# Attention and gated FFN on one core: slots by inner tile with four accumulators open, two batches in turns at the start, one order by hand

## The chip, the cores and the metric

The kernel runs on one core of a Trainium2 chip. The metric is the device time of one execution in microseconds (us). Engines are called as in the profile: PE does matmuls (PEld loads their weights), DVE is the vector engine, ACT the scalar engine, POOL the general one, SP issues most DMAs.

## What is computed

Eight batches of eight heads, 576 tokens of 64 elements, 32 memories per head, then a feed-forward part on all 4608 tokens with model width 512 and inner width 2048:

```python
a = exp(phi - max(phi)); a = a / (sum(a) + 1e-09)
k_m = einsum('bhsm,bhsd->bhmd', a, k)
v_m = einsum('bhsm,bhsd->bhmd', a, v)
scores = (q @ k_m^T) / 8
attn = softmax(scores)                 # with + 1e-09 in the sum
x = (attn @ v_m) as (4608, 512)
h = x @ w_in
out = (h * clip(h + 3, 0, 6) / 6) @ w_out
```

The two weight matrices reach the core as 64-bit floats.

## The kernel before

**Tiles.** A batch is handled in two halves (hf) of 256 and 320 tokens. The inner width is cut into 16 tiles f of 128; four of them are a chunk c of w_in (w1), and w_out (w2) has one piece per tile. Per batch the attention makes the memories (`pk`), turns them (`pq`), makes scores (`psc`) and probabilities (`phi`, `plo`: high and low part). `fold` (L308) multiplies the value memories with a chunk of w1 into `pv`, and `unload` (L325, L326) splits this into high and low parts, `both`, two tiles f at a time.

**A slot** is one half and one tile f: `gemm1` (L357) makes `ph` with six matmuls; `gate` makes `gf` (ACT L370, then DVE L371, with a 64-column piece for tokens beyond 256, L374, kept in `rest`), then its high part `ghi` (ACT L377) and low part `glo` (DVE L384); `gemm2` (L398) adds six products with w2 to two accumulators `acc`. gemm2 runs two slots behind gemm1 (LAG = 2). On the second half of every second batch, the kept 64-token pieces of two batches make a third tile, `rboth`, with three more matmuls a slot and a third accumulator. There are two PSUM buffers for `ph`, four for `acc` and one pair for the attention.

**Weights.** Each piece of 128 x 512 double words becomes 32-bit floats: ACT makes the size and shifts the low word (L95, L96), DVE clamps, shifts and masks (L102 to L104), POOL adds the integers (L105). A w2 piece is then split into high (ACT L110) and low (POOL L111). Converted chunks of w1 are written to DRAM (`w1_kept`) and fetched back for later batches.

**Order.** The last seven batches stand in an order written by hand: all 16 tiles of the first half, then of the second, and the next batch's attention steps at fixed slots, run as `aside` between ghi and glo. The first batch is different. Only SP's loads are in a fixed order there (`FETCH`). `SCRIPT` (attention and first weights) and `PLAN` (slots, weight pieces by `tick`, steps of batch 1) say in which order the work is recorded, and a scheduler with an estimate of times decides how it stands on each engine. It runs the first batch as four rows of eight slots: each half over tiles 0 to 7, kept as partial sums in DRAM, then each over 8 to 15. Batch 1's slots follow when batch 0 is finished.

Of the kernel before, what the change touches and what calls it, by code (L numbers as in the profile page):

```python
# [33 lines left out]
PLAN = ('0.0 13 C1 w2 - - / 0.1 - w3 E1 / 0.2 / 0.3 w4 / 0.4 F1 D1 / 0.5 w5 w6 / 0.6 B1 R1 - w7 21 / 0.7 - / 1.0 23 / 1.1 - 20 - 22 - / 1.2 / 1.3 / 1.4 / 1.5 w8 w9 - / 1.6 31 - - / 1.7 30 F2 - w11 32 - 33 S - / 2.8 / 2.9 S w10 w12 F3 / 2.10 S S / 2.11 - / 2.12 S S - w13 - S - S S S / 2.13 S - w14 w15 G0 / 2.14 S - - / 2.15 S / 3.8 / 3.9 S / 3.10 - G1 G2 S S S / 3.11 - / 3.12 / 3.13 G3 S - S S / 3.14 / 3.15'
)
SCRIPT = ('maxima / tick 00 01 / exponents / memories (0,1) / memories (2,3,4) / normalise / turn / scores 0 / centre 0 / tick 02 03 - / exponent 0 / divide 0 / tick w0 w1 / tick 10 @scores0 / back 0 / tick 12 @divide0 / tick 11 @centre0 / rest 0 / scores 1 @back0 / fold 0'
)
FETCH = ('pt 00 k2 k0 pn k1 k3 01 03 k4 02 w0 q0 w1 10 11 13 q1 w2 20 12 w3 w4 w6 w11 w5 w9 23 w10 w7 21 22 w8 31 30 w15 32 w12 w14 33 w13'
)
HOT = lambda hf: hf == 0  # L40
GLO = lambda ch, f: False
# [9 lines left out]


@with_exitstack
def attention_ffn_kernel(ctx: ExitStack, tc: tile.TileContext, pn, pt, kv, qt, w1, w2, out):
# [30 lines left out]

    def halves(raw):
        words = raw.bitcast(U32).rearrange("p (n t) -> p n t", t=2)
        return words[:, :, 0], words[:, :, 1]  # L90

    def begin(raw):
        low, high = halves(raw)
        tmp = sb.tile([P, DM], U32, name="tmp", **TMP)
        nc.scalar.activation(tmp.bitcast(F32), high.bitcast(F32), AF.Abs)  # L95
        nc.scalar.activation(low, low, AF.Copy, scale=2.0**-29)  # L96
# [2 lines left out]
    def join(raw, tmp, dst):
        low, high = halves(raw)  # L100
        size = tmp.bitcast(F32)
        nc.vector.tensor_scalar(size, size, LOW, TOP, ALU.max, ALU.min)  # L102
        nc.vector.tensor_scalar(tmp, tmp, 3, 0x3FFFFFF8, ALU.logical_shift_left, ALU.bitwise_and)  # L103
        nc.vector.scalar_tensor_tensor(high, high, 0xC0000000, tmp, ALU.bitwise_and, ALU.bitwise_or)  # L104
        nc.gpsimd.tensor_tensor(tmp if dst is None else dst, high, low, ALU.add)  # L105

    def split(f, full):
        w2_sb[f] = wpool.tile([P, 2, DM], F32R, name=f"w2_{f}", tag=f"w2_{f}")
        hi, lo = w2_sb[f][:, 0], w2_sb[f][:, 1]
        nc.scalar.copy(hi, full)  # L110
        nc.gpsimd.tensor_tensor(lo, full, hi.bitcast(F32), ALU.subtract)  # L111
# [549 lines left out]
```

## Time and profile before

| | |
|---|---|
| time, median of 3 runs | 765.0 us (763.57 to 766.19) |
| the profiled execution | 766.2 us |
| its span | 764.3 us |
| busy: PE / DVE / ACT / POOL | 701.9 / 440.6 / 369.3 / 119.5 us |
| bytes read / written in HBM | 86.52 / 14.69 MB |

A page of the profile comes from one execution. Times in a row are the start from the beginning of the span and the duration; in a group's row the total busy time and the mean of one in ns, then how long the engine stood idle before these instructions, and what ended that. An fp32 matmul shows as two instructions. `L` numbers are lines of the kernel; the changed kernel's lines are other ones.

### The profile page before, as it was taken

How to read it: one execution, taken by the hardware profiler on the slowest of the kernel's cores; microseconds unless marked ns; L12 is line 12 of the kernel's file. 1: busy time of each engine (PE TensorE's matmuls, PEld its weight loads, DVE VectorE, ACT ScalarE, POOL GpSimd, SP SyncE). 2: the span in 40 equal slices, each digit the busy share in tenths (PEclk: the TensorE clock that was granted, in tenths of full speed). 3: DMA queues.
4: the chain of work that ended last, by engine and by line, in shares of the span. 5: the costliest groups of instructions: out<-in, count | busy, mean ns of one | idle time of the engine just before them, and what ended most of it. 6: DMA issues, size and time to landing. Idle time of an engine off the chain costs nothing.

```text
span 764.3 us, 12420 instructions
## 1 busy us (share of the span) xinstructions
PE 701.9 (92%) x4690; PEld 563.4 (74%) x4690; DVE 440.6 (58%) x1033; ACT 369.3 (48%) x823; POOL 119.5 (16%) x99
## 2 busy tenths in 40 slices
...
PEclk9559999999999999999999999999999999999999
...
GB/s 324 409 406 48 283 169 277 140 257 12 248 109 86 97 111 194 117 106 45 240 93 85 97 139 195 108 95 69 227 77 82 152 3 82 56 28 1 29 1 41
DMA packets 28442, 102.00 MB, mean 133 GB/s; under 512 B 4960, under 2 KB 5856, under 8 KB 24288
## 3 DMA queue, kind: packets, MB, share of 16 engines
...
q8 instruction: 37, 0.61, 0.3%
...
HBM read 86.52 MB, written 14.69 MB: 132 GB/s over the span
## 4 chain that ended last, share of the span: by engine, by line
PE 79%; DMA 8%; DVE 8%; issue 2%; ACT 2%; POOL 1%; SPq 0%; POOLq 0%; DVEq 0%; ACTq 0%
PE acc L398 48%; PE ph L357 24%; PE pv L308 3%; DMA raw<-in_w 3%; PE pk L225 2%; DVE raw L104 2%; DVE tmp L102 1%; DMA kvt<-in_kv 1%; DMA nmx<-nmx 1%; PE psc L254 1%; DVE tmp L103 1%; DMA w<-w_kept 1%; DVE glo L384 1%; DMA ptile<-in_pt 1%; POOL w L105 1%
## 5 line engine op out<-in xcount | busy, mean ns | idle before, releaser
L398 PE MATMUL acc<-w,ghi 128*128 128x512 f32 x1024 | 288.7, 401 | 0.8 <-POOL w L111 0.6
L370 ACT ACTIVATE gf<-ph,three 128x320 f32<-128x320 f32 (+1 forms) x256 | 128.0, 500 | 200.1 <-PE ph L357 195.6
L371 DVE SCALAR_TENSOR_TENSOR gf<-gf,ph 128x256 f32<-128x256 f32 x256 | 107.0, 418 | 199.0 <-ACT gf L370 198.4
L398 PEld LDWEIGHTS acc<-w,ghi 128*128 128x128 f32 x1024 | 178.7, 189 | 54.4 <-ACT gf L370 23.2
L357 PEld LDWEIGHTS ph<-phi,both 128*128 128x128 f32 x1024 | 165.4, 191 | 54.6 <-DVE gf L371 15.8
L357 PE MATMUL ph<-phi,both 128*128 128x320 f32 (+1 forms) x1024 | 182.6, 300 | 23.0 <-DVE gf L371 11.2
L377 ACT CAST ghi<-gf 128x256 fp32r<-128x256 f32 x256 | 104.0, 406 | 144.5 <-DVE gf L371 144.3
L398 PE MATMUL acc<-w,glo 128*128 128x512 f32 x512 | 165.4, 399 | 1.9 <-DVE glo L384 1.9
L384 DVE TENSOR_TENSOR glo<-gf,ghi 128x256 fp32r<-128x256 f32 x256 | 114.1, 447 | 48.3 <-ACT ghi L377 47.1
L398 PEld LDWEIGHTS acc<-w,glo 128*128 128x128 f32 x512 | 95.6, 189 | 28.7 <-DVE glo L384 3.7
L357 PE MATMUL ph<-plo,both 128*128 128x320 f32 (+1 forms) x512 | 110.4, 297 | 0.0
L357 PEld LDWEIGHTS ph<-plo,both 128*128 128x128 f32 x512 | 83.3, 191 | 0.0
L273 POOL TENSOR_TENSOR st<-st,mx 128x640 f32<-128x640 f32 (+1 forms) x15 | 18.5, 1235 | 387.0 <-DVE mx L272 387.0
L326 DVE TENSOR_TENSOR both<-pv,both 128x512 fp32r<-128x512 f32 x64 | 44.1, 689 | 45.8 <-ACT both L325 45.7
L398 PE MATMUL acc<-w,rboth 128*128 128x512 f32 x192 | 54.9, 394 | 0.0
L308 PE MATMUL pv<-w,kvT 64*32 64x512 f32 x512 | 39.7, 629 | 8.7 <-DVE st L263 5.8
L398 PEld LDWEIGHTS acc<-w,rboth 128*128 128x128 f32 x192 | 36.1, 188 | 9.0
L325 ACT CAST both<-pv 128x512 fp32r<-128x512 f32 x64 | 37.1, 580 | 5.5 <-DVE both L326 4.9
L225 PE MATMUL pk<-kvt,pnat 128*32 128x129 f32 (+1 forms) x640 | 22.1, 289 | 9.4 <-DVE pnat L215 4.4
L104 DVE SCALAR_TENSOR_TENSOR raw<-raw,tmp 128x512 uint32<-128x512 uint32 x32 | 30.5, 957 | 0.3
L225 PEld LDWEIGHTS pk<-kvt,pnat 128*32 128x32 f32 (+1 forms) x640 | 18.2, 115 | 12.8 <-ACT pnat L216 5.1
L95 ACT ACTIVATE tmp<-raw 128x512 f32<-128x512 f32 x32 | 21.1, 674 | 13.1 <-DMA raw<-in_w 7.7
...
## 6 DMA issues: line engine op xcount, KB each, us to landing
...
```

The lines of the kernel that those rows point to most:

```text
L95: nc.scalar.activation(tmp.bitcast(F32), high.bitcast(F32), AF.Abs)
L104: nc.vector.scalar_tensor_tensor(high, high, 0xC0000000, tmp, ALU.bitwise_and, ALU.bitwise_or)
L225: nc.tensor.matmul(self.pk[j * M : (j + 1) * M, g, :KV], self.pnat[:rows, t, g * P + j * M : g * P + (j + 1) * M], kvt[:rows, g * NJ + j, ...
L308: nc.tensor.matmul(pv[j * M : (j + 1) * M, g, :], self.kvT[rows, g, j * M : (j + 1) * M], w1_sb[c][rows, j, :].bitcast(F32), start=True, s ...
L325: nc.scalar.copy(vhi, pv[:, :, x : x + VC])
L326: nc.vector.tensor_tensor(vlo, pv[:, :, x : x + VC], vhi.bitcast(F32), ALU.subtract)
L357: nc.tensor.matmul(ph, w[:, g, fs], x[:, g * n : (g + 1) * n], start=(i == 0), stop=(i == len(seq) - 1),)
L370: nc.scalar.activation(gf, ph, AF.Relu, bias=three)
L371: nc.vector.scalar_tensor_tensor(gf[:, :n], gf[:, :n], 6.0, ph[:, :n], ALU.min, ALU.mult)
L377: nc.scalar.copy(ghi, gf[:, :n])
L384: nc.vector.tensor_tensor(glo, gf[:, :n], ghi.bitcast(F32), ALU.subtract)
L398: nc.tensor.matmul(accs[a], lo if i == 2 else hi, w2lo if i == 1 else w2hi, start=(first and i == 0), stop=(last and i == 2),)
```

## The change

1. **Slots by inner tile.** From batch 2 on, a batch runs tile by tile, both halves of a tile after each other (`pairs`), so that two halves of two accumulators are open at once. LAG is 3. The third accumulator is gone: after every second batch a `rest_segment` of its own makes eight double tiles of the kept pieces, with one accumulator.
2. **First two batches in turns.** Batch 0 runs tiles 0 to 3 half by half (FIRST, 8 slots), batch 1 tiles 0 to 3 half by half and 4 to 7 in pairs (SECOND, 16 slots), batch 0 tiles 4 to 15 (THIRD, 24 slots), batch 1 tiles 8 to 15 (FOURTH, 16 slots). The partial sums of both batches go to DRAM and come back (`keep`, `recall`).
3. **One order by hand.** The whole kernel stands under `manual_schedule`: each engine gets its instructions in the order in which the code records them. A table names the work of each slot's aside; `begin`, `size`, `join` and `split` are the steps of a weight unit, `unfold` is one half of unload.
4. **Weight units of 1024 columns** in place of pieces of 512. The integer add is recorded on DVE (`nc.vector`), no longer on POOL. Two buffers `tmp` of 1024 columns take the place of four of 512.
5. **Small things.** Five matmuls without use (`warm`) in the prologue; the second half's scores of batch 0 go to two accumulator buffers (`scoreb`); the transposed scores are read when centre runs; phi, plo and kvT have other buffer counts; output goes out in larger DMAs.

```diff
-LAG = 2
-PLAN = ('0.0 13 C1 w2 - - / 0.1 - w3 E1 / 0.2 / 0.3 w4 / 0.4 F1 D1 / 0.5 w5 w6 / ...
-SCRIPT = ('maxima / tick 00 01 / exponents / memories (0,1) / ...
+LAG = 3
+PROLOGUE = """
+pt.0 raw.0.0 pn.0 kv.0 raw.0.1 q.0.0 raw2.0 max.0 q.0.1 raw2.1
+begin.0.0.0 size.0.0.0 join.0.0.0 exps.0 mem.0 norm.0 turn.0 begin.0.0.1 size.0.0.1
+score.0.0 pt.1 pn.1 kv.1 centre.0.0 exp.0.0 join.0.0.1 scoreb.0.1 q.1.0 warm.4 begin.1.0 div.0.0 back.0.0
+fold.0.0 unfold.0 rest.0.0 warm.1
+"""
+FIRST = """
+0 unfold.0 size.1.0 / 1 join.1.0 split.0 max.1 spread.1 q.1.1 raw2.2 raw2.3 / 2 centre.0.1 exp.0.1
+/ 3 div.0.1 back.0.1 rest.0.1 begin.1.1 / 4 size.1.1 exps.1 / 5 join.1.1 split.1 mem.1
+/ 6 norm.1 turn.1 raw.1.0 raw.1.1 score.1.0 centre.1.0 exp.1.0 fold.1.0
+/ 7 unfold.1 div.1.0 back.1.0 unfold.1 rest.1.0
+"""
+SECOND = """
...
+/ 8 unfold.1 size.1.2 / 9 join.1.2 split.2 begin.1.3 / 10 size.1.3 / 11 join.1.3 split.3 begin.0.2.0
...
+THIRD = """
+0 begin.1.4 / 1 size.1.4 / 2 join.1.4 / 3 split.4 fold.0.2 unfold.0 / 4 unfold.0 begin.0.3.0 / 5 size.0.3.0 / 6 join.0.3.0
...
+    def begin(*u):
+        sizes[u] = sb.tile([P, UNIT], U32, name="tmp", **TMP)
+        for cols, high, part in raw[u]:
+            nc.scalar.activation(sizes[u][:, cols].bitcast(F32), high.bitcast(F32), AF.Abs)
+            nc.scalar.activation(part, part, AF.Copy, scale=2.0**-29)
...
-        nc.vector.scalar_tensor_tensor(high, high, 0xC0000000, tmp, ALU.bitwise_and, ALU.bitwise_or)
-        nc.gpsimd.tensor_tensor(tmp if dst is None else dst, high, low, ALU.add)
...
+            nc.vector.scalar_tensor_tensor(size_, high, 0xC0000000, size_, ALU.bitwise_and, ALU.bitwise_or)
+            nc.vector.tensor_tensor(dst[:, cols], size_, part, ALU.add)
...
+    def split(u):
...
+        nc.scalar.copy(w2_sb[u][:, 0], whole)
+        nc.gpsimd.tensor_tensor(w2_sb[u][:, 1], whole, w2_sb[u][:, 0].bitcast(F32), ALU.subtract)
...
+    def high_low(aside, *sources):
...
+        nc.scalar.copy(ghi, src)
+        aside()
+        nc.vector.tensor_tensor(glo, src, ghi.bitcast(F32), ALU.subtract)
...
+        segment(0, halves(range(4)), table(FIRST, atts), keep)
+        segment(1, halves(range(4)) + pairs(range(4, 8)), table(SECOND, atts), keep)
+        segment(0, pairs(range(4, NFT)), table(THIRD, atts), store)
+        segment(1, pairs(range(8, NFT)), table(FOURTH, atts), store)
+        for b in range(2, B + 1):
+            if b % 2 == 0:
+                rest_segment(b - 1, {})
```

Three places show how the instructions stand on the engines. The first is ACT among the weights of w2: before, in the first batch's slots.

```order
L110 CAST w_5_570<-tmp 128x512
L377 CAST ghi<-gf 128x256
L96 ACTIVATE raw<-raw 128x512
L370 ACTIVATE gf<-ph,three 128x256
L95 ACTIVATE tmp<-raw 128x512
L377 CAST ghi<-gf 128x256
L110 CAST w_6_577<-tmp 128x512
L370 ACTIVATE gf<-ph,three 128x256
```

And now, in slots 9 and 10 of SECOND (relu is L384, ghi L376, split L154, begin L127 and L128):

```order
L384 ACTIVATE gf<-ph,three 128x320
L376 CAST ghi<-gf 128x256
L154 CAST w_2_892<-tmp 128x1024
L127 ACTIVATE tmp<-raw_3_333 128x1024
L128 ACTIVATE raw_3_333<-raw_3_333 128x1024
L384 ACTIVATE gf<-ph,three 128x256
L376 CAST ghi<-gf 128x256
```

Single pieces of 512 columns stood between relu and ghi of several slots; now all of a unit's ACT work stands between one slot's ghi and the next slot's relu. The second place is the beginning of DVE's program, before:

```order
L194 TENSOR_REDUCE nmx<-ptile 128x2
L202 TENSOR_SCALAR diag<-ident,nmx 128x128 x2
L102 TENSOR_SCALAR tmp<-tmp 128x512
L103 TENSOR_SCALAR tmp<-tmp 128x512
L104 SCALAR_TENSOR_TENSOR raw<-raw,tmp 128x512
L215 TENSOR_TENSOR pnat<-pnat,pa 128x512 x2
L215 TENSOR_TENSOR pnat<-pnat,pa 128x256
```

Now (size is L132 and L133, join L145 and L146, the exponents' addition L230):

```order
L209 TENSOR_REDUCE nmx<-ptile 128x2
L217 TENSOR_SCALAR diag<-ident,nmx 128x128 x2
L132 TENSOR_SCALAR tmp<-tmp 128x1024
L133 TENSOR_SCALAR tmp<-tmp 128x1024
L145 SCALAR_TENSOR_TENSOR tmp<-raw,tmp 128x512
L146 ISA w_136<-raw,tmp 128x1024
L145 SCALAR_TENSOR_TENSOR tmp<-raw,tmp 128x512
L146 ISA w_136<-raw,tmp 128x1024
L230 TENSOR_TENSOR pnat<-pnat,pa 128x512 x2
L230 TENSOR_TENSOR pnat<-pnat,pa 128x256
```

Two pieces with their adds stand ahead of the exponents in place of one without; the add of 512 words is listed as an ISA instruction of 1024 elements. The third place is PE at batch 1's memories, before (they stood among batch 0's last tiles):

```order
L357 MATMUL ph<-phi,both 128x256 x2
L357 MATMUL ph<-plo,both 128x256 x2
L225 MATMUL pk<-kvt,pnat 32x129 x40
L357 MATMUL ph<-phi,both 128x256 x4
L357 MATMUL ph<-plo,both 128x256 x2
L398 MATMUL acc<-w_12_1051,ghi 128x512 x4
```

Now, in slots 5 and 6 of FIRST (gemm1 is L361, gemm2 L443, the memories L239):

```order
L361 MATMUL ph<-phi,both 128x320 x4
L361 MATMUL ph<-plo,both 128x320 x2
L239 MATMUL pk<-kvt,pnat 32x129 x40
L443 MATMUL acc<-w_1_437,ghi 128x512 x4
L443 MATMUL acc<-w_1_437,glo 128x512 x2
L361 MATMUL ph<-phi,both 128x320 x4
L361 MATMUL ph<-plo,both 128x320 x2
L259 MATMUL pq<-ident,kvn 128x128 x2
```

The memories moved from the end of batch 0 to its sixth slot, and the acc of tile 2, which reads the second w2 unit, stands ahead of the next ph.

More of the change, by code (lines that the diff above doesn't have):

```diff
@@ L30 @@
 FC = DF // NCHUNK
+FPC = FC // P
+UNIT = 2 * FC
 KV = 2 * D + 1
 EPS = 1e-9
-LAG = 2
[L34 to L41, printed above, removed]
+LAG = 3
 VC = 256
-VW_RING = {"tag": "vw", "bufs": 9}
-TMP = {"tag": "tmp", "bufs": 4}
+VW_RING = {"tag": "vw", "bufs": 6}
+TMP = {"tag": "tmp", "bufs": 2}
+O_RING = {"tag": "o", "bufs": 2}
 WIDE = {"tag": "wide", "bufs": 2}
@@ L99, in join @@
[L99 to L111, printed above, removed]
@@ new lines, in store_rest, with finish @@
+    def store_rest(b, hf, accs):
+        o = sb.tile([P, 2, DM], F32, name="o", **O_RING)
+        half = DM // 2
+        nc.scalar.mul(o[:, 0, :half], accs[0][:, :half], 1.0 / 6.0)
+        nc.vector.tensor_scalar(o[:, 0, half:], accs[0][:, half:], 1.0 / 6.0, None, ALU.mult)
+        for k in range(2):
+            row = (b + k) * S - REST
+            nc.sync.dma_start(out=out[row : row + REST], in_=o[k * REST : (k + 1) * REST, 0])
+    pending = []
+    open_accs = {}
+    def finish(key, tiles, first, last, end):
+        if first:
+            open_accs[key] = [bank() for _ in range(1 + max(t[0] for t in tiles))]
+        accs = open_accs[key]
+        one = len(accs) == 1
+        order = [(k, i) for i in range(3) for k in range(len(tiles))]
+        if not one and last:
+            order.sort()
+        for n, (k, i) in enumerate(order):
+            a, hi, lo, f = tiles[k]
+            w2hi, w2lo = w2_parts(f)
+            opens = n == 0 if one else i == 0
+            closes = n == len(order) - 1 if one else i == 2
@@ L603, in attention_ffn_kernel @@
-    then = ahead(2)
-    with tc.manual_schedule():
-        for b in range(1, B):
-            att, nxt = nxt, then
-            rows, then = timetable(nxt, b + 2)
-            for hf in range(2):
-                def aside(f):
-                    for what in rows[hf * NFT + f]:
-                        what()
-                run(b, hf, range(NFT), store, None, None, None, aside)
+                start=first and opens,
+                stop=last and closes,
+            )
+        if last:
+            end(*key, open_accs.pop(key))
```

504 lines of the change are left out of this document (207 added, 297 removed).

## The prediction

> **What bounds the kernel now.** I read the page first, then the busy time of each engine by stages, then single rows of the stages that matter.
>
> ```profile
> span 764.3 us, 12420 instructions
> PEclk9559999999999999999999999999999999999999
> 0.00:54.00 54.00, 15.80 (x160) 8.11 (x160) 40.58 (x68) 29.57 (x51) 20.70 (x23) 0.67 0.99 381
> 54.00:126.00 72.00, 57.22 (x336) 41.61 (x336) 66.94 (x115) 46.10 (x95) 41.51 (x31) 0.96 0.57 189
> 126.00:185.00 59.00, 54.02 (x429) 40.90 (x423) 37.27 (x82) 26.18 (x60) 11.36 (x9) 0.97 0.60 171
> 270.00:441.00 171.00, 171.00 (x1188) 139.91 (x1192) 90.61 (x232) 81.11 (x186) 15.32 (x12) 1.00 0.43 122
> ```
>
> The columns of a stage are its length, then busy time of PE, PEld, DVE, ACT and POOL, the granted clock, the DMA share and GB/s. From 270 to 441 us PE is never idle at clock 1.00. Before 54 us it works 15.8 us of 54 and at a mean clock of 0.67; from 54 to 126 us DVE is busy 66.9 us of 72 and PE 57.2. So there is a start of some 185 us, short of data first and then of DVE, and after it PE alone sets the pace.
>
> ```profile
> 269.90 2.54 PE L225 MATMUL pk<-kvt,pnat 128*32 128x129 f32 x80
> 440.56 2.54 PE L225 MATMUL pk<-kvt,pnat 128*32 128x129 f32 x80
> 137.12 0.74 PE L357 MATMUL ph<-phi,both 128*128 128x320 f32 x4
> 139.40 0.75 PE L357 MATMUL ph<-phi,both 128*128 128x320 f32 x4
> 158.82 0.64 PE L357 MATMUL ph<-phi,both 128*128 128x256 f32 x4
> 160.93 0.64 PE L357 MATMUL ph<-phi,both 128*128 128x256 f32 x4
> 758.96 0.87 PE L398 MATMUL acc<-w,rboth 128*128 128x512 f32 x3
> ```
>
> Two batches take 440.56 - 269.90 = 170.7 us, so eight at PE's pace take 682.6. The last matmul ends at 759.8, which leaves a tail of 4.5. The start therefore loses 764.3 - 682.6 - 4.5 = **77 us**, and only that can change: the matmuls of the eight batches are the same in number and shape. A slot (one inner tile of one half: six matmuls into ph, six into acc) costs PE 139.40 - 137.12 = 2.28 us with 320 columns and 160.93 - 158.82 = 2.11 with 256, so 2.2 on average; of it the six acc matmuls are about 1.4.
>
> **The change, part by part.** The steady part keeps its folds, attention steps and matmuls; PE hides ACT (81 us of 171) and DVE (91 of 171) there. I cost its new order, the separate rest tiles and the longer delay of three slots at nothing; were that cover gone, each slot could cost up to the 1.35 us that follows below.
>
> What matters is one order written by hand for the start. In it every engine works through its instructions in program order, and one slot's chain is:
>
> ```profile
> 243.88 0.53 ACT L370 ACTIVATE gf<-ph,three 128x320 f32<-128x320 f32 x1 [1.36 <-PE ph L357]
> 244.43 0.42 DVE L371 SCALAR_TENSOR_TENSOR gf<-gf,ph 128x256 f32<-128x256 f32 x1 [1.46 <-ACT gf L370]
> 244.89 0.41 ACT L377 CAST ghi<-gf 128x256 fp32r<-128x256 f32 x1 [0.48 <-DVE gf L371]
> 245.33 0.42 DVE L384 TENSOR_TENSOR glo<-gf,ghi 128x256 fp32r<-128x256 f32 x1 [0.34 <-ACT ghi L377]
> ```
>
> From relu to gf 0.55 us, from there to ghi 0.46; with 0.35 until ACT is free, the next relu can start 1.35 us after the last. A slot's extra work now stands between ghi and the next relu on ACT, and between gf and glo on DVE. So a slot with extra ACT work a takes 1.35 + a, one with extra DVE work d about 0.9 + d (gf, the 64-column piece, glo), and where ACT's extra work waits for DVE's, both add up. A waiting cast holds up the next relu and through it everything on DVE, hence the next ph bank and PE. In the old order weight pieces of 512 columns overlapped freely on ACT, DVE and POOL.
>
> The weight pieces, alone and by group:
>
> ```profile
> 43.18 0.67 ACT L95 ACTIVATE tmp<-raw 128x512 f32<-128x512 f32 x1 [1.17 <-DVE raw L104]
> 43.76 0.66 ACT L96 ACTIVATE raw<-raw 128x512 uint32<-128x512 uint32 x1
> 48.05 0.41 DVE L103 TENSOR_SCALAR tmp<-tmp 128x512 uint32<-128x512 uint32 x1
> 48.39 0.41 DVE L102 TENSOR_SCALAR tmp<-tmp 128x512 f32<-128x512 f32 x1
> 7.70 0.69 DVE L104 SCALAR_TENSOR_TENSOR raw<-raw,tmp 128x512 uint32<-128x512 uint32 x1
> L104 DVE SCALAR_TENSOR_TENSOR raw<-raw,tmp 128x512 uint32<-128x512 uint32 x32 | 30.5, 957 | 0.3
> L105 POOL TENSOR_TENSOR w<-raw 128x512 uint32<-128x512 uint32 x16 | 19.9, 1246 | 36.0 <-DVE raw L104 30.7 <-PE ph L357 4.1 <-ACT st L276 1.1
> L111 POOL TENSOR_TENSOR w<-tmp,w 128x512 fp32r<-128x512 f32 x16 | 23.6, 1479 | 8.3 <-ACT w L110 8.3
> ```
>
> The change converts units of 1024 columns. Back to back, ACT starts a 512-column op every 0.58 us and DVE a tensor_scalar every 0.34. No row shows 1024 columns; one op must lie between one and two halves, and I take nearly two: begin 2.0 us on ACT (2.3 for w1, still in halves), size 1.2 on DVE. The mask-and-or is 0.61 per half back to back. The integer add moves from POOL to DVE as another kind of instruction. No row shows it there: below it is bounded by a 0.41 pass over 512 columns, above by POOL's own 1.25; I take 0.75, near the 0.69 of L104 on the same operands. So join is 2.7 us for w1 and, in one piece, 2.6 for w2. split is 0.95 on ACT and then 2.6 on POOL, under two of L111's 1.48 since one start is saved. Moving the add takes 37 us off POOL and lets DVE's passes run nearer 0.69 than the group's 0.957; I have counted that gain by pricing DVE without POOL beside it.
>
> The beginning, before any slot:
>
> ```profile
> 6.07 0.67 ACT L95 ACTIVATE tmp<-raw 128x512 f32<-128x512 f32 x1 [4.06 <-DMA raw<-in_w]
> 10.45 1.62 DVE L215 TENSOR_TENSOR pnat<-pnat,pa 128x512 f32<-128x512 f32 x3 [2.06 <-DMA pnat<-in_pn]
> 12.28 3.19 PE L225 MATMUL pk<-kvt,pnat 128*32 128x129 f32 x64 [4.42 <-DVE pnat L215]
> 18.33 1.08 PE L225 MATMUL pk<-kvt,pnat 64*32 64x129 f32 x16 [2.87 <-DMA kvt<-in_kv]
> 19.47 0.16 DVE L236 TENSOR_SCALAR rs<-pk 128x2 f32<-128x2 f32 x1 [2.91 <-PE pk L225]
> 22.97 1.11 PE L254 MATMUL psc<-qh,kvT 64*32 64x256 f32 x16 [0.67 <-ACT kvT L247]
> 53.95 0.41 DVE L371 SCALAR_TENSOR_TENSOR gf<-gf,ph 128x256 f32<-128x256 f32 x1
> ```
>
> Now DVE converts half of the first w1 chunk ahead of the exponents. ACT starts its first piece at 6.07 as before, the second lands 1.3 us later (512 KB at 381 GB/s), so size and join run from 7.9 to 12.0, so the exponents start at 12.0 instead of 10.45. But the last key tile no longer waits behind weights, and pk (4.3 us) ends near 17.5 instead of 19.4. From rs to psc 3.5 us less ACT work that went between: psc at 20.1. Then on DVE size to 23.1, transpose, maximum and subtraction to 25, join to 27.7, division to 29.8, transpose to 30.5; phi on ACT, fold, one half of both and plo to 33.7, and the first gf at **34.5** against 53.95 (the old one came after many pieces that could have waited). The warm matmuls run on PE beside that DVE chain. By pk (40 products of 129 columns, four side by side, in 2.54 us: 2.0 ns a column) one is 1.0 us, twice that at half clock; without this cover the four would cost 4 to 8 us.
>
> On SP the start's loads (ptile, half a w1 chunk, pnat, kv, the other half, q, w2 unit 0, q, w2 unit 1: 9 MB, 24 us at 381 GB/s) stand in the order of use and land before it. Behind batch 1's row of maxima and its way through DRAM wait a q and two w2 units, needed over ten slots later; all other pieces are issued at least six slots ahead. I cost SP and DMA at nothing; a piece that came late would hold ACT's begin and so the gate by as much.
>
> Then the slots, priced with these parts. The two halves' attention adds round trips through POOL inside one slot:
>
> ```profile
> L282 DVE TENSOR_REDUCE sm<-st 128x20 f32<-128x640 f32 x8 | 6.5, 811 | 0.5 <-ACT st L276 0.5
> L285 POOL TENSOR_TENSOR st<-st,sm 128x640 f32<-128x640 f32 x8 | 10.3, 1290 | 21.9 <-DVE sm L284 20.5 <-ACT gf L370 1.4
> L289 DVE STREAM_TRANSPOSE pT<-st 128x640 f32<-128x640 f32 x8 | 6.7, 837 | 0.2
> L298 POOL TENSOR_TENSOR plo<-pT,phi 128x640 fp32r<-128x640 f32 x8 | 12.7, 1590 | 16.0 <-ACT phi L292 16.0
> ```
>
> Division and turning back in one slot: 0.34 + 0.81 + 0.45 (the two small ops) + 1.29 on POOL + 0.84 + phi 0.7 + plo 1.59, then the end of ph 0.45 and 0.55 to the next gf: **7.0 us**, since the next half's first ph needs plo. There are three such slots (7.05, 7.8 with two unfolds, 7.0). A slot with norm, turn, score and centre chained through PE takes 7.3.
>
> - FIRST, 8 slots: 3.55 + 4.6 + 4.7 + 7.05 + 4.3 + 9.0 + 7.3 + 7.8 = 48.3. The 9.0 is a join and split (4.7) after which PE's acc of slot 2 waits 4.3 more for POOL's low half of the second w2 unit, ahead of the next ph.
> - SECOND, 16 slots: 3.65, 2.2, 2.75, 7.0, 3.9, 2.05, 3.55, 3.9, 3.55, 6.7, 1.9, 7.0, 1.9, 4.4, 3.55, 3.5 = 61.5. The 6.7 is slot 9: 0.5 + join 2.6 + 0.1 + split 0.95 + begin 2.0 + 0.55.
> - THIRD, slots 0 to 18: six units of w2 and w1 in turns of begin (3.35 to 4.65), size (2.05), join (3.4) or join with split (4.7): 61.0. After slot 18 no weights are left and PE sets the pace.
>
> First gf 34.5 + 48.3 + 61.5 + 61.0 = 205.3 us. PE, which runs ahead of gf by one ph and is behind in acc by one tile, has then done 42 slots (92.2), three more ph (2.4), six folds at 1.33 (8.0, what is left of 170.7 us after slots, rest tiles and attention) and two batches' memories and scores (8.3): 110.9 of the 682.6. The rest follows at PE's pace: 205.3 + 571.7 + 4.5 = **781.5 us** of span, 17 more than before. The profiled execution took 766.2, 1.9 more than its span, and the median shown, 765.0, is 1.2 under that: 781.5 + 1.9 - 1.2 = 782.
>
> **A rule against the change.** The clock row above shows two slices of 19 us at half clock although PE worked in them; later there is one short fall:
>
> ```profile
> 160.00:180.00 20.00, 15.51 (x131) 11.23 (x133) 11.09 (x23) 8.85 (x21) 0.00 (x0) 0.91 0.40 148
> ```
>
> The Trainium skill, "TensorE: Matmul & The Clock Gate", Part 1, says that the clock falls to half after an idle window of about 3.4 us and rises after a busy one. The trace agrees in part: 0.91 over 20 us is 3.6 us at half. By that rule the warm matmuls help once and each wait of 7 us lets the clock fall again, which is the third rival below.
>
> **The rivals.**
> - *DVE and ACT overlap* (faster): if the chain did not add up and each stage took only its DVE work, FIRST would take 31 us (eight gates 7.8, two w2 units 8.8, attention, unfolds and the store 14), SECOND 51, THIRD 57: 173.5 at the end of 48 slots with 119.6 done, so 741 of span, 742 as a median. It is decided where the mean slot up to there falls below 3.6 us (mine is 4.0); for it speaks DVE's 67 of 72 us in the old stage, against it the program order of both engines. Half of that effect would be about no change.
> - *The add is dear*: at 1.25 per half, 28 halves on the path add 14 us: 796. At 0.41 they take 9.5 away: 773. The order lists it with twice its columns, which speaks for dear.
> - *The clock falls at each long wait*: six waits, each followed by about 1.5 slots at double time, cost up to 6 x 2 = 12 us: 794. For it speaks the fall between 160 and 180 us, against it that this one cost only 3.6 us at half clock.
> - *The early start is all*: stalls no larger than before after the first gf, 19 us earlier: 746. Against it: the chain above.
>
> **How the numbers follow.** Forecast near 782 (770 to 790): 0.47. The add or the clock dearer (790 to 806): 0.20. Faster, by overlap or by the early start (738 to 762): 0.27. No change: 0.06. The range from 744 to 800 leaves out half of the dear end and some of the fast one. Within 0.3% (2.3 us) is what a measurement of this kernel tells from no change: faster 0.27, same 0.06, slower 0.67.
>
> **What would show it.** The first gf near 34 us; gf of the 44th slot near 205; PE busy well under half its time from 35 to 80 us; ACT relus released by casts that wait for DVE's add; from about 210 us on the old pace of 170.7 us for two batches. The forecast is wrong if the add is under 0.5 us per half, if the 1024-column ops cost little more than 512, or if slots of the SECOND stage average under 3.2 us.

## The result and the profile after

| | changed | before, on the same chip |
|---|---|---|
| time, median | 817.6 us (816.2 to 818.7) | 764.6 us (763.6 to 766.2) |
| ratio | 1.069, 95% interval 1.066 to 1.072 | |
| span of the profiled execution | 814.3 us | 764.3 us |
| busy: PE / DVE / ACT / POOL | 721.2 / 434.5 / 362.4 / 77.9 us | 701.9 / 440.6 / 369.3 / 119.5 us |

The direction was forecast, the size was not: 782 us, and at most 800. From the page of the changed kernel, its span and the granted clock in 40 slices:

```profile
span 814.3 us, 12199 instructions
PEclk9756888999989999999999999999999999999999
```

The clock is now below nine tenths of full speed not in two slices but in six of the first ten, and in one later. The busy times by stage, changed kernel (length, PE, PEld, DVE, ACT, POOL, granted clock, DMA share, GB/s):

```profile
35.00:80.00 45.00, 25.80 (x170) 16.91 (x169) 21.75 (x41) 15.36 (x29) 10.33 (x6) 0.62 0.43 148
80.00:140.00 60.00, 45.46 (x225) 34.19 (x224) 35.59 (x69) 28.68 (x53) 10.83 (x7) 0.83 0.37 140
140.00:210.00 70.00, 53.33 (x290) 40.59 (x290) 50.67 (x97) 39.31 (x75) 7.63 (x4) 1.00 0.41 142
210.00:255.00 45.00, 33.10 (x251) 26.46 (x252) 22.20 (x51) 15.71 (x36) 2.38 (x1) 0.89 0.47 105
330.00:500.00 170.00, 167.01 (x1150) 137.10 (x1156) 89.14 (x222) 77.95 (x174) 14.21 (x11) 1.00 0.33 112
```

Three things stand in these rows. Up to 140 us no engine is the bound: PE, DVE and ACT all work well under their time, so instructions wait for one another. From 210 to 255, where PE was expected to set the pace, it works 33 of 45 us. And in the steady part it is idle 3 us in 170, where it was never idle before. The gate of the first slot of each table, and of the 44th slot, in the timeline of the changed kernel:

```profile
35.15 0.42 DVE L385 SCALAR_TENSOR_TENSOR gf<-gf,ph 128x256 f32<-128x256 f32 x1 [1.10 <-ACT gf L384]
...
90.39 0.42 DVE L385 SCALAR_TENSOR_TENSOR gf<-gf,ph 128x256 f32<-128x256 f32 x1 [1.11 <-ACT gf L384]
...
153.82 0.41 DVE L385 SCALAR_TENSOR_TENSOR gf<-gf,ph 128x256 f32<-128x256 f32 x1
...
216.16 0.42 DVE L385 SCALAR_TENSOR_TENSOR gf<-gf,ph 128x256 f32<-128x256 f32 x1 [1.21 <-ACT gf L384]
```

So FIRST took 55.2 us (forecast 48.3), SECOND 63.4 (61.5), slots 0 to 18 of THIRD 62.3 (61.0), and the first gate came 0.7 late. The 44th slot came at 216.2 instead of 205.3: 10.9 us of the error. From there to the end it took 598.2 us, where 571.7 + 4.5 were forecast: the other 22.0.

### The profile page after: what moved, and what is told of

Same layout as the page of the kernel before. It is cut to its first block, busy times and chain, and to the rows that moved or that the text cites. A ratio compares the mean times of both kernels' runs of the same rounds, so it can differ in the third digit from the quotient of the medians.

```text
span 814.3 us, 12199 instructions
## 1 busy us (share of the span) xinstructions
PE 721.2 (89%) x4700; PEld 575.4 (71%) x4700; DVE 434.5 (53%) x997; ACT 362.4 (45%) x765; POOL 77.9 (10%) x59
## 4 chain that ended last, share of the span: by engine, by line
PE 71%; DVE 13%; ACT 6%; issue 5%; DMA 3%; POOL 2%; SPq 0%; DVEq 0%; ACTq 0%; POOLq 0%
PE acc L443 42%; PE ph L361 21%; PE pv L334 3%; PE pk L239 3%; DVE tmp L145 2%; DVE gf L385 2%; DMA raw<-in_w 2%; DVE glo L378 2%; ACT tmp L127 1%; DVE tmp L132 1%; PE psc L273 1%; ACT gf L384 1%; DMA nmx<-nmx 1%; DVE tmp L146 1%; ACT raw L128 1%
## 5 line engine op out<-in xcount | busy, mean ns | idle before, releaser
L443 PE MATMUL acc<-w,ghi 128*128 128x512 f32 x1152 | 330.8, 406 | 12.4 <-ACT w L154 6.3
L443 PEld LDWEIGHTS acc<-w,ghi 128*128 128x128 f32 x1152 | 204.6, 192 | 78.6 <-issue 29.1
L361 PE MATMUL ph<-phi,both 128*128 128x320 f32 (+1 forms) x1024 | 186.3, 305 | 42.3 <-DVE rest L388 17.6
L361 PEld LDWEIGHTS ph<-phi,both 128*128 128x128 f32 x1024 | 167.4, 193 | 73.7 <-ACT gf L384 18.1
L384 ACT ACTIVATE gf<-ph,three 128x256 f32<-128x256 f32 (+1 forms) x256 | 127.7, 499 | 166.1 <-PE ph L361 165.2
L443 PE MATMUL acc<-w,glo 128*128 128x512 f32 x576 | 187.6, 402 | 0.3 <-DVE glo L378 0.3
L376 ACT CAST ghi<-gf 128x256 fp32r<-128x256 f32 x256 | 104.1, 407 | 166.8 <-DVE gf L385 166.8
L378 DVE TENSOR_TENSOR glo<-gf,ghi 128x256 fp32r<-128x256 f32 x256 | 111.8, 437 | 49.4 <-ACT ghi L376 48.4
L443 PEld LDWEIGHTS acc<-w,glo 128*128 128x128 f32 x576 | 110.6, 192 | 26.5 <-DVE glo L378 0.8
L361 PE MATMUL ph<-plo,both 128*128 128x256 f32 (+1 forms) x512 | 112.2, 301 | 0.6 <-POOL plo L326 0.4
L361 PEld LDWEIGHTS ph<-plo,both 128*128 128x128 f32 x512 | 84.0, 193 | 1.9 <-POOL plo L326 1.6
L239 PE MATMUL pk<-kvt,pnat 128*32 128x129 f32 (+1 forms) x640 | 23.4, 302 | 17.9 <-issue 11.1
L239 PEld LDWEIGHTS pk<-kvt,pnat 128*32 128x32 f32 (+1 forms) x640 | 19.6, 121 | 22.2 <-issue 14.5
L155 POOL TENSOR_TENSOR w<-tmp,w 128x1024 fp32r<-128x1024 f32 x8 | 19.3, 2409 | 148.5 <-ACT w L154 148.5
L388 DVE SCALAR_TENSOR_TENSOR rest<-gf,ph 128x64 f32<-128x64 f32 x128 | 27.5, 214 | 0.0
L231 ACT ACTIVATE pnat<-pnat 128x512 f32<-128x512 f32 (+1 forms) x24 | 13.2, 559 | 27.5 <-DVE pnat L230 27.2
L326 POOL TENSOR_TENSOR plo<-pT,phi 128x640 fp32r<-128x640 f32 (+1 forms) x15 | 21.6, 1437 | 20.3 <-ACT phi L321 20.3
```

Of the source, the lines that this page charges most:

```text
L239: nc.tensor.matmul(self.pk[j * M : (j + 1) * M, g, :KV], self.pnat[:rows, t, g * P + j * M : g * P + (j + 1) * M], kvt[:rows, g * NJ + j, ...
L326: self.aux[hf].tensor_tensor(plo, self.pT, phi.bitcast(F32), ALU.subtract)
L361: nc.tensor.matmul(ph, w[:, g, fs], x[:, g * n : (g + 1) * n], start=(i == 0), stop=(i == len(seq) - 1),)
L376: nc.scalar.copy(ghi, src)
L378: nc.vector.tensor_tensor(glo, src, ghi.bitcast(F32), ALU.subtract)
L384: nc.scalar.activation(gf, ph, AF.Relu, bias=three)
```

## The experiments

Each was timed beside the kernel before on the same chip; "changed" is the 817.6 us. The chip was not the same for all: the kernel before took from 764.6 to 766.9 us, so a difference of 2 us between two experiments says little, and their ratios say more.

### The maxima of batch 2

The timeline of the changed kernel where THIRD passes into FOURTH:

```profile
222.63 0.38 SPq L213 DMA_DIRECT2D nmx<-nmx  x1
223.06 0.46 SPq L403 DMA_DIRECT2D o<-partial  x1
231.33 0.32 SPq L225 DMA_DIRECT2D nmxb<-nmx  x1
...
236.47 0.69 DVE L230 TENSOR_TENSOR pnat<-pnat,nmxb 128x512 f32<-128x512 f32 x1 [10.63 <-DMA nmxb<-nmx]
237.08 0.42 DVE L378 TENSOR_TENSOR glo<-gf,ghi 128x256 fp32r<-128x256 f32 x1
```

The maxima stand in slot 21 of THIRD, their row goes to DRAM and comes back spread over the partitions, and the exponents that need it stand in slot 0 of FOURTH, three slots later. DVE waits 10.63 us, with the next glo, and so acc, queued behind. In the steady table the maxima stand in slot 22, their spreading in 26 and the exponents in slot 3 of the next batch of 32 slots, 13 slots after the maxima. The edit:

```diff
-/ 14 unfold.0 begin.1.6 size.1.6 / 15 join.1.6 split.6 / ... / 21 max.2 recall.0.1 / 22 spread.2 q.2.1
+/ 14 unfold.0 begin.1.6 size.1.6 max.2 / 15 join.1.6 split.6 spread.2 / ... / 21 recall.0.1 / 22 q.2.1
```

> Against the changed kernel's 817.6 us: the maxima of batch 2 stand in slot 14 of THIRD instead of 21 and their way through DRAM starts in slot 15 instead of 22; nothing else moves. Theory 1 (the 10.6 us that DVE waits for nmxb at the start of FOURTH is on the path): the wait goes, slot 48 falls from 12.85 us to about 3, and the time falls by 8 to 12 us, to 806 to 810. Rival (DVE's wait only takes the place of another that ends as late, PE's own work or the memories' loads): the wait goes and the time stays within 2 us of 817.6.

Measured: 806.3 us (ratio to before 1.052, 1.050 to 1.055), 11.3 less than the changed kernel, as the first theory said. The same row, with the gate ahead of it, in this kernel's timeline:

```profile
227.15 0.42 DVE L385 SCALAR_TENSOR_TENSOR gf<-gf,ph 128x256 f32<-128x256 f32 x1 [0.56 <-ACT gf L384]
227.49 0.68 DVE L230 TENSOR_TENSOR pnat<-pnat,nmxb 128x512 f32<-128x512 f32 x1
```

The wait is gone, and slot 48 takes 2.4 us instead of 12.85. The wait was on the path with its whole length.

### The folds of the steady part

The timeline of the changed kernel ahead of a batch's memories:

```profile
310.77 0.69 DVE L349 TENSOR_TENSOR both<-pv,both 128x512 fp32r<-128x512 f32 x1 [0.95 <-ACT both L348]
...
311.57 2.54 PE L239 MATMUL pk<-kvt,pnat 128*32 128x129 f32 x80 [1.51 <-issue]
```

And the waits of the same kernel (total, times, longest):

```profile
PE pk L239 <- issue: 11.1, 6, 3.6
```

The 3.6 us are batch 2's pk in FOURTH; the other five are the steady part's, about 1.5 us each. The view calls it "issue", but pk starts 0.11 us after DVE has read the second half of `pv`: both use the one pair of banks. In the changed kernel's table the second fold stands in slot 5, its unloads in 5 and 6, the memories in 7.

```diff
-2 fold.C.1 unfold.C / 3 unfold.C exps.N.0 / 4 exps.N.1 / 5 exps.N.2 fold.C.2 unfold.C / 6 unfold.C / 7 mem.N
+1 fold.C.1 unfold.C / 2 unfold.C exps.N.0 / 3 exps.N.1 / 4 exps.N.2 fold.C.2 unfold.C / 5 unfold.C / 7 mem.N
```

> Against the changed kernel's 817.6 us: in the steady table the folds of chunks 1 and 2 with their unloads, and the exponents, stand one slot earlier; the memories stay in slot 7. Theory 1 (the memories' matmuls wait for the one pair of accumulation banks until DVE has read the fold's second half): the 1.75 us before each of six pk groups goes to about 0.2, and the time falls by 8 to 10 us, to 808 to 810. Rival (PE waits there for its instructions, which are fetched near those times): the gap before pk stays 1.7 us and the time stays within 2 us of 817.6.

Measured: 810.6 us (1.058, 1.056 to 1.061), 7.0 less, a little under the 8 to 10 expected; the steady part has five such places, not six. The same place in this kernel:

```profile
311.11 0.69 DVE L349 TENSOR_TENSOR both<-pv,both 128x512 fp32r<-128x512 f32 x1 [0.83 <-ACT both L348]
312.44 2.54 PE L239 MATMUL pk<-kvt,pnat 128*32 128x129 f32 x80
```

pk follows without a pause, although its instructions are the same in the same slot: the pair of banks was the cause, not their fetching. Nor was it the exponents, which moved too: in the changed kernel the last of them ended at 307.96, 3.6 us before pk. Two batches take 170.6 us from gate to gate instead of 173.7, which is the old pace (170.7). So LAG 3, pairs and the separate rest tiles cost nothing, as forecast; only this one neighbourhood did.

> The two edits of the runs before in one kernel: maxima of batch 2 earlier and the steady folds earlier. Theory 1 (two separate causes, one at the start of FOURTH and one in each steady batch): the gains add, 817.6 - 11.3 - 7.0 = 799 us, within 2. Rival (both gains come from the same slack, as when the steady part only waits for something that FOURTH left late): 804 to 808.

Measured with both edits: 798.1 us (1.042, 1.039 to 1.044), 19.5 less. The gains add (11.3 + 7.0 is 18.3, and 799 was expected). From the 44th gate to the end it now takes 578.4 us of the 576.2 forecast, so the two edits explain 19.8 of those 22.0.

### The clock

21 matmuls that nobody reads, in slots 1, 2, 3, 5 and 6 of FIRST, where PE waits:

```diff
-1 join.1.0 split.0 max.1 spread.1 ... / 2 centre.0.1 ... / 3 div.0.1 ... / 5 ... mem.1 / 6 norm.1 turn.1 ...
+1 warm.4 join.1.0 split.0 max.1 spread.1 ... / 2 warm.4 centre.0.1 ... / 3 warm.4 div.0.1 ... / 5 ... mem.1 warm.6 / 6 norm.1 warm.3 turn.1 ...
```

> Against the changed kernel's 817.6 us: 21 matmuls whose result nothing reads are added to slots 1, 2, 3, 5 and 6 of FIRST, into a bank that is free, where PE waits. Theory 1 (of the 7 us by which FIRST came out above the forecast, most is PE at half clock): the granted clock in 35 to 80 us goes from 0.62 to above 0.85, FIRST from 55.2 to 47 to 50 us, and the time falls by 5 to 9 us, to 809 to 813. Rival (FIRST is bound by the chain on DVE, ACT and POOL, and PE's clock does not matter): the clock rises and FIRST stays within 2 us of 55.2, the time within 2 us of 817.6, or above it where the added matmuls delay PE.

Measured: 820.1 us (1.069, 1.066 to 1.072). The window from 35 to 80 us of this kernel:

```profile
35.00:80.00 45.00, 37.26 (x221) 22.37 (x220) 21.98 (x42) 15.10 (x29) 10.34 (x6) 0.92 0.43 148
```

The clock rose from 0.62 to 0.92, and FIRST took 53.8 us instead of 55.2. That is worth 1.5 us there, a fifth of FIRST's surplus, and the time did not fall at all. By the end of THIRD 1.9 us were won, but in the profiled execution the first gate came 1.2 us later, FOURTH took 1.5 longer and the first eight slots of batch 2 took 2.9 longer; the edit touches none of these places, and what lengthened them stays open. So in FIRST a low clock was in the main a sign of waiting, not its cause. The later stages were not tried.

### The add, and POOL beside DVE

The add of every unit back on POOL:

```diff
-            nc.vector.tensor_tensor(dst[:, cols], size_, part, ALU.add)
+            nc.gpsimd.tensor_tensor(dst[:, cols], size_, part, ALU.add)
```

> Against the changed kernel's 817.6 us: the integer add of every weight unit goes back from DVE to POOL, all else as it is. Theory 1 (on DVE the add costs 1.22 us in a slot, on POOL about 2.4, and DVE's operations with two inputs in SBUF wait while POOL works: those beside POOL's took 36 us over their medians in the kernel before and 5 in the changed one): slots with join and split get 1.2 us longer, others lose 1.2 on DVE and get part of it back by waits; 820 to 835 us. Rival (POOL is idle and hides the add): about ten join slots lose 1.2 us each, 803 to 810.

Measured: 826.6 us (1.078, 1.076 to 1.081), 9.0 more than changed. The groups of the weights' steps by form, changed kernel first:

```profile
L155 POOL TENSOR_TENSOR w<-tmp,w 128x1024 fp32r<-128x1024 f32 x8 | 19.3, 2409 | 148.5 <-ACT w L154 148.5
L146 DVE CUSTOM_DVE_ANT_0 w<-raw,tmp 128x1024 uint16<-128x1024 uint16 x16 | 11.1, 692 | 0.8
L146 DVE CUSTOM_DVE_ANT_0 tmp<-raw,tmp 128x2048 uint16<-128x2048 uint16 x8 | 9.8, 1225 | 0.3
L145 DVE SCALAR_TENSOR_TENSOR tmp<-raw,tmp 128x1024 uint32<-128x1024 uint32 x8 | 9.7, 1218 | 0.0
L127 ACT ACTIVATE tmp<-raw 128x1024 f32<-128x1024 f32 x8 | 9.1, 1138 | 0.0
```

With the add on POOL:

```profile
L146 POOL TENSOR_TENSOR w<-tmp,raw 128x512 uint32<-128x512 uint32 x16 | 24.1, 1526 | 48.4 <-ACT gf L384 16.5 <-DVE tmp L145 15.3 <-ACT st L305 13.1
L146 POOL TENSOR_TENSOR tmp<-tmp,raw 128x1024 uint32<-128x1024 uint32 x8 | 19.5, 2434 | 55.5 <-DVE tmp L145 43.8 <-ACT ghi L376 11.7
```

On DVE the add takes 0.69 us for 512 columns (listed with twice its columns) and 1.23 for 1024, on POOL 1.53 and 2.43. Slots with join and split got 1.3 us longer, as expected (slot 9 of SECOND 6.45 to 7.81). In this table the add on DVE is worth 9 us.

The other work on POOL in the first two batches, and the low halves of w2 units 0 to 3, to DVE:

```diff
-            self.aux = [nc.vector if b == 0 and hf == 0 else nc.gpsimd for hf in range(2)]
+            self.aux = [nc.vector if b < 2 else nc.gpsimd for hf in range(2)]
...
-        nc.gpsimd.tensor_tensor(w2_sb[u][:, 1], whole, w2_sb[u][:, 0].bitcast(F32), ALU.subtract)
+        (nc.vector if u < 4 else nc.gpsimd).tensor_tensor(w2_sb[u][:, 1], whole, w2_sb[u][:, 0].bitcast(F32), ALU.subtract)
```

> Against the changed kernel's 817.6 us: in batches 0 and 1 the subtraction, division and low half of the second half's (and batch 1's) attention go from POOL to DVE (0.69 to 0.84 us instead of 1.05 to 1.56), and so do the low halves of w2 units 0 to 3 (about 1.22 instead of 2.4). Theory 1 (these round trips stand in series in their slots): FIRST falls by about 4 us from 55.2, SECOND by about 3 from 63.4, the time to 808 to 812. Rival (DVE is the longer chain there, and more work on it delays its slots as much): within 2 us of 817.6, or above.

Measured: 817.4 us (1.067, 1.065 to 1.069): no gain. Slots 2, 3 and 5 of FIRST fell by 0.7, 1.1 and 1.6 us. But slot 1 rose by 2.4: the low half is now in DVE's queue ahead of glo, where DVE waits 1.17 us for the cast and then works 1.23. And slot 4 rose by 1.0: the row of maxima, behind that low half, came later, and DVE waited 0.96 us for it. A faster engine shortens a slot where the slot only waits for that step, and lengthens one where the step's own wait then holds what is queued behind it.

### Weights in pieces

Each operation of a unit in a slot of its own, in SECOND and THIRD, with a third `tmp`; `begin` is cut into `abs` and `scl`, `join` into `sgn` and `add`:

```diff
-/ 8 unfold.1 size.1.2 / 9 join.1.2 split.2 begin.1.3 / 10 size.1.3 / 11 join.1.3 split.3 begin.0.2.0
+/ 8 unfold.1 sgn.1.2 / 9 abs.1.3 add.1.2 / 10 split.2 size.1.3 / 11 scl.1.3 sgn.1.3
```

> Against the changed kernel's 817.6 us: in SECOND and THIRD each unit's two ACT operations, its two-step size, its or and its add stand in slots of their own instead of begin and join as a whole in one slot, with a third tmp buffer; the operations are the same. Theory 1 (a slot costs 1.35 us and its extra ACT work, or 0.9 us and its extra DVE work, in series, where that is above PE's 2.2): SECOND falls from 63.4 to about 51 us and slots 0 to 20 of THIRD from 67 to about 57, so 12 to 22 us in all, 796 to 806. Rival (the weights' total work bounds these segments, or a slot's work in pieces costs as much in waits between engines): within 4 us of 817.6.

Measured: 813.2 us (1.061, 1.058 to 1.064), 4.3 less. SECOND fell to 60.3 us, not 51; slots 0 to 19 of THIRD from 64.7 to 62.7. Slots 9 and 10 of SECOND came to 2.3 us each, but some took far more. Slot 11 of SECOND, 6.0 us, in this kernel's timeline:

```profile
132.40 2.43 POOL L169 TENSOR_TENSOR w<-tmp,w 128x1024 fp32r<-128x1024 f32 x1 [22.94 <-ACT w L168]
...
133.25 2.67 DVE L150 SCALAR_TENSOR_TENSOR tmp<-raw,tmp 128x1024 uint32<-128x1024 uint32 x1
...
134.89 1.22 PE L457 MATMUL acc<-w,ghi 128*128 128x512 f32 x2 [1.78 <-POOL w L169]
```

Two waits stand here. PE waits for POOL's low half with its acc, and the next ph is queued behind. And DVE's mask-and-or, 1.22 us alone, takes 2.67: it ends 1.1 us after POOL does, as if it had not begun before. So the low halves of units 2 to 7 went to DVE (`hi.2 size.1.3 lo.2` in place of `split.2 size.1.3`, and so on):

> The kernel with pieces (813.2 us), whose gain was a third of what was expected, with one more edit: the low halves of w2 units 2 to 7 on DVE behind the slot's other DVE work instead of on POOL. In its trace two slots took 6.0 us (SECOND 11, THIRD 15): PE's acc waited 1.8 us for POOL's low half, and a DVE mask-and-or beside POOL's operation took 2.67 us where it takes 1.22 alone. Theory 1 (POOL's low half holds both PE and DVE there): these two slots go to 3.5 to 4, others gain at most 1.2 where DVE is the shorter, and the time to 807 to 811 us. Rival (the added DVE work, 6 x 1.22, gives it back): 812 us or above.

Measured: 810.8 us (1.057, 1.054 to 1.060). Slot 11 of SECOND took 3.7 us and slot 15 of THIRD 3.2, SECOND 57.6 in all, but FOURTH, where nothing was edited, 69.3 instead of 67.6. That POOL's low half held these slots is shown; the edit takes both waits away at once, so it does not tell them apart. The time is at the upper end of the 807 to 811 expected: a gain of only 2.4 us, and the two ratios' intervals overlap, so a gain in time is not shown.

### All of it written anew

```diff
+FIRST = """
+0 unfold.0 max.1 spread.1 centre.0.1 q.1.1 raw2.2 raw2.3 / 1 exp.0.1 sgn.1.0 add.1.0 / 2 hi.0 div.0.1 abs.1.1 back.0.1 lo.0 scl.1.1
+/ 3 exps.1 rest.0.1 mem.1 size.1.1 sgn.1.1 / 4 norm.1 add.1.1 turn.1 hi.1 lo.1 raw.1.0 raw.1.1 / 5 score.1.0 centre.1.0
+/ 6 exp.1.0 fold.1.0 div.1.0 unfold.1 / 7 back.1.0 unfold.1 rest.1.0 abs.0.1.0 score.1.1
...
```

> Everything together: FIRST, SECOND and THIRD are written anew so that no slot holds more than about two of the weights' operations and no operation stands in the slot of the one it waits for; batch 1's maxima stand in slot 0 of FIRST and its memories in 3 instead of 5, batch 2's maxima in slot 16 of THIRD; nothing of batches 0 and 1 runs on POOL; steady folds one slot earlier; a third tmp buffer. Theory 1 (slots are priced by the longer of 1.35 us plus ACT's and 0.95 plus DVE's extra work, and chains in series add): FIRST 37 to 42 us, SECOND 46 to 50, THIRD 60 to 64, FOURTH 53 to 56, the time 740 to 760 us, below the kernel before. Rival (as with the pieces alone, waits of PE for low halves and folds give back two thirds of it): 775 to 785 us.

Measured: 775.1 us (1.011, 1.008 to 1.013), 42.5 less than changed but not below the kernel before. SECOND took 51.0 us, THIRD 67.1, but FIRST still 48.4, and the time is the rival's 775, not the 740 to 760 of the first theory. Two slots of FIRST held chains still (slot 3 with 11.8 us, slot 7 with 9.1), and the next kernel went after five places:

> From the trace of the kernel written anew before (775.05 us), five places that a chain still held: in FIRST the exponents waited for the row of maxima (nmxb landed at 51.92) and PE stood with the memories ahead of its acc and ph (slot 3, 11.8 us), and the scores of batch 1's second half waited for the fold's second half to be read (slot 7, 9.1 us); folds ahead of their unloads in one slot (three slots of 4.0 to 4.4 us); the fold at the start of FOURTH with two exponents (4.1 and 3.8 us). Here batch 1's maxima come first in slot 0, the memories stand in slot 4, those scores go to two free banks, folds stand one slot before their unloads, and FOURTH's fold stands in slots 21 to 23 of THIRD, where PE was ahead. Theory 1 (each of them is a wait of its own): FIRST 48.4 to 38 to 41 us, SECOND 51 to 49, THIRD 67 to 65 to 68, FOURTH 55.5 to 51 to 52; 757 to 763 us, below the kernel before on the same chip. Rival (DVE's total work bounds the start by now, and what one slot gives up the next takes): 769 to 775 us.

Measured: 775.9 us (1.013, 1.010 to 1.015): nothing won. FIRST and FOURTH fell by 2.2 and 3.4 us as meant, but two of the moves made new waits. The fold put into slot 21 of THIRD found the pair still unread, and PE, with acc and ph behind, stood; the maxima of batch 3, one slot later, held SP's queue, the output DMAs behind them came late, and the rest tiles waited for their buffer. In this kernel's timeline:

```profile
197.57 1.12 PE L350 MATMUL pv<-w,kvT 64*32 64x512 f32 x16 [2.66 <-DVE both L365]
...
272.80 0.38 ACT L436 ACTIVATE o<-acc 128x256 f32<-128x256 f32 x1 [4.03 <-DMA out_t<-o]
```

This execution took 780.3 us, the slowest of six with a median of 775.9, so the wait of 4.03 us may be shorter in the others. The next kernel put the fold into slot 23, the maxima back into slot 14, and pulled three more chains apart:

```diff
-/ 3 rest.0.1 size.1.1 sgn.1.1 exps.1 / 4 add.1.1 hi.1 mem.1 lo.1 raw.1.0 raw.1.1 / 5 norm.1 turn.1 score.1.0
+/ 3 rest.0.1 size.1.1 sgn.1.1 exps.1 / 4 add.1.1 hi.1 mem.1 lo.1 norm.1 raw.1.0 raw.1.1 / 5 turn.1
-/ 6 centre.1.0 exp.1.0 fold.1.0 / 7 div.1.0 scoreb.1.1 back.1.0 unfold.1 rest.1.0 unfold.1 abs.0.1.0
+/ 6 score.1.0 centre.1.0 fold.1.0 unfold.1 exp.1.0 / 7 div.1.0 scoreb.1.1 back.1.0 unfold.1 rest.1.0 abs.0.1.0
...
```

> From the trace of the last kernel (775.9 us): memories with norm in slot 4 and the turn alone in 5 (slot 5 took 7.7 us because acc and ph stood on PE behind the chain norm, turn, scores); a fold stands at least one slot behind the add that it waits for, and ahead of its acc otherwise as before (slot 4 of THIRD took 4.0 us for a size of 1.4); the cast to hi and the low half of one unit in two slots (two slots of 4.4 us); batch 2's second fold in slot 23 of THIRD instead of 21, where PE stood 2.7 us and fell to half clock (slot 4.9 us); batch 3's maxima back in slot 14 of FOURTH (a wait of 4.2 us in batch 2). Theory 1 (each place was a wait of its own): FIRST 40 to 43 us, SECOND 48 to 50, THIRD 62 to 65, FOURTH 52 to 54, two batches 170.6; 757 to 763 us, below the kernel before. Rival (what one slot gives up the next takes, as in the last run): 768 to 776 us.

Measured: 763.6 us (0.997, 0.995 to 0.999), just outside the 757 to 763 expected. Slot 5 of FIRST fell from 7.7 to 2.75 us, FIRST to 40.8, SECOND came to 50.5 and THIRD to 66.1. The last kernel halves the first warm matmuls and moves batch 2's maxima to slot 10 of THIRD and its exponents into slots 21 to 23:

```diff
-score.0.0 ... q.1.0 warm.4 begin.1.0 div.0.0 back.0.0
+score.0.0 ... q.1.0 warm.2 begin.1.0 div.0.0 back.0.0
...
-/ 21 lo.7 recall.0.1 / 22 q.2.1 / 23 fold.1.3
+/ 21 exps.2.0 lo.7 recall.0.1 / 22 exps.2.1 q.2.1 / 23 fold.1.3 exps.2.2
```

> From the kernel before this in the series (763.59 us): two places. The warm matmuls stood on PE from 27.6 to 32.4 us ahead of the first fold, whose pv could start only at 32.3 though the weights were there at 27.4: here two instead of four. Batch 2's three exponents stood in slots 0 to 2 of FOURTH beside the unloads and batch 0's store (3.8 and 4.1 us): here its maxima stand in slot 10 of THIRD and the exponents in 21 to 23, where DVE had room. Theory 1: the first gf 1.5 us earlier, FOURTH 1.5 to 2.5 us shorter, THIRD up to 1 us longer, 760 to 762 us, 0.5 to 0.8% under the kernel before. Rival (with fewer warm matmuls PE is at half clock at the first gates and FIRST takes as much longer): 763 to 765.

Measured: **761.0 us** (0.992, 0.989 to 0.994), 56.6 less than changed and 0.8% below the kernel before. Its span and the gates of the first and the 44th slot:

```profile
span 759.7 us, 12173 instructions
...
33.99 0.41 DVE L401 SCALAR_TENSOR_TENSOR gf<-gf,ph 128x256 f32<-128x256 f32 x1
...
180.93 0.42 DVE L401 SCALAR_TENSOR_TENSOR gf<-gf,ph 128x256 f32<-128x256 f32 x1 [1.04 <-ACT gf L400]
```

The first gate came 2.7 us earlier than in the kernel before it in the series; FIRST to FOURTH together took the same (212.0 against 211.5 us). That this is due to the warm matmuls fits, but the first gate lies anywhere from 34.9 to 37.3 us in kernels with the same warm matmuls, so it isn't shown. The stages side by side, from the gates (FOURTH to the first gate of batch 2, with the rest tiles):

| us | forecast | changed | both edits | anew, first | third | fourth |
|---|---|---|---|---|---|---|
| first gf | 34.5 | 35.2 | 35.0 | 35.0 | 36.7 | 34.0 |
| FIRST | 48.3 | 55.2 | 55.0 | 48.4 | 40.8 | 40.6 |
| SECOND | 61.5 | 63.4 | 63.3 | 51.0 | 50.5 | 51.5 |
| THIRD | | 71.6 | 72.7 | 67.1 | 66.1 | 66.9 |
| FOURTH | | 67.3 | 55.6 | 55.5 | 54.1 | 53.0 |
| two batches | 170.7 | 173.7 | 170.6 | 170.7 | 170.7 | 170.6 |

## Why the prediction missed

**What held.** The first gate (35.2 for 34.5), the price of the add (0.69 us for 0.75) and of split (1.05 and 2.41 us for 0.95 and 2.6), and the rule that a slot's extra work stands in the chain of its gates: SECOND and THIRD came within about 3% in all (SECOND's dear slots 3, 9 and 11 took 7.9, 6.5 and 6.7 us for 7.0, 6.7 and 7.0). Some of that is luck: SECOND's slots 0 to 3 took 2.7 us more than priced and the others 0.8 less, and where the same rule priced the weights in pieces it was 9 us too low for SECOND (60.3 for 51). That the early first gate would be given back is right too. One sign did not come: PE was busy not well under half of its time from 35 to 80 us but 57% of it, in part with matmuls at half clock.

**"I cost SP and DMA at nothing": 11 us.** The prediction looked at what waits behind batch 1's row of maxima, in FIRST, and not at batch 2's, which the new table puts three slots ahead of its use. Undoing that alone gave 11.3 us.

**"I cost its new order ... at nothing": 7 us.** PE's cover hides ACT and DVE in the steady part, but not a wait of PE itself: the second fold and the memories share one pair of banks, and the fold's last unload and the memories stood one slot apart. Undoing it gave 7.0 us. The order of the rest, the delay and the rest tiles cost nothing, as said.

**FIRST, 48.3, was 6.9 us short.** By slots, from the gates:

| slot | 0 | 1 | 2 | 3 | 4 | 5 | 6 | 7 |
|---|---|---|---|---|---|---|---|---|
| forecast | 3.55 | 4.6 | 4.7 | 7.05 | 4.3 | 9.0 | 7.3 | 7.8 |
| measured | 3.65 | 4.35 | 4.85 | 7.96 | 4.51 | 10.77 | 10.66 | 8.49 |

Slots 5 and 6 hold 5.1 of the 6.9. Their chain in the timeline of the changed kernel:

```profile
63.44 1.04 ACT L154 CAST w<-tmp 128x1024 fp32r<-128x1024 f32 x1 [2.12 <-DVE tmp L146]
64.54 0.73 PE L443 MATMUL acc<-w,ghi 128*128 128x512 f32 x2 [2.60 <-ACT w L154]
64.57 2.35 POOL L155 TENSOR_TENSOR w<-tmp,w 128x1024 fp32r<-128x1024 f32 x1 [10.22 <-ACT w L154]
66.97 1.22 PE L443 MATMUL acc<-w,ghi 128*128 128x512 f32 x2 [1.69 <-POOL w L155]
...
72.77 0.69 PE L259 MATMUL pq<-ident,kvn 128*128 128x128 f32 x2 [2.13 <-ACT kvn L254]
73.92 1.11 PE L273 MATMUL psc<-qh,kvT 64*32 64x256 f32 x16 [0.46 <-ACT kvT L261]
75.91 1.96 PE L334 MATMUL pv<-w,kvT 64*32 64x512 f32 x16 [0.87 <-DVE st L286]
77.80 1.22 PE L443 MATMUL acc<-w,ghi 128*128 128x512 f32 x2
...
80.26 0.75 PE L361 MATMUL ph<-phi,both 128*128 128x320 f32 x4
...
81.34 0.53 ACT L384 ACTIVATE gf<-ph,three 128x320 f32<-128x320 f32 x1 [1.27 <-PE ph L361]
```

Slot 6 was priced by the attention chain alone, 7.3. But PE too takes its instructions in order: behind pq, psc and pv stand acc and the next ph (77.8 to 81.3), and the next relu comes after them. That term, some 3 us, was left out. Pulling this chain apart (norm in slot 4, scores in 6) took slot 5 of the later kernels from 7.7 to 2.75 us, with slots 4 and 6 as long as before; this shows the mechanism, though in a table written anew and not in the changed kernel. The clock, the rival with the clock gate, is 1.5 us of the surplus by the run with more matmuls. The surplus of slot 5 (1.8 us), where half clock also stretches acc and ph, has no run of its own.

**The sum.** 10.9 us up to the 44th gate and 19.8 by the two edits make 30.7 of the 32.8 us by which the span was missed. The other 2.1 are not settled by a run of their own. A part of them may be the pair of banks once more: in the kernel with both edits batch 2's memories in FOURTH wait 1.33 us and start 0.10 us after DVE has read the half of the fold that stands one slot ahead:

```profile
233.83 0.69 DVE L349 TENSOR_TENSOR both<-pv,both 128x512 fp32r<-128x512 f32 x1 [0.96 <-ACT both L348]
...
234.62 2.54 PE L239 MATMUL pk<-kvt,pnat 128*32 128x129 f32 x80 [1.33 <-issue]
```

In the last kernel, where that fold stands in THIRD, this wait is gone. The rest may lie in FOURTH's slots 1 and 2, with a fold, two exponents and a store (4.1 and 3.8 us in the kernel with both edits; 3.5 and 2.4 in the last).

**The rivals.** "The add is dear" fell by its row. "The clock falls at each long wait" was right about the clock and, in FIRST, wrong about the price (1.5 us; SECOND and THIRD were not tried). "Overlap" fell: the mean slot up to the 44th gate took 4.2 us, not under 3.6, and slots got short only when the table was rewritten. "The early start is all" was wrong by 72 us.
